# A second gate with its weights in four column groups of TensorE, and expert blocks nested in each other

## The chip, the core and the metric

The kernel runs on one core of one Trainium2 chip. The core has five engines, each with its own queue of instructions: TensorE (PE; PEld is its loading of weights), VectorE (DVE), ScalarE (ACT), GpSimd (POOL) and SyncE (SP, which here issues loads and stores). They wait for each other by semaphores. The metric is the device time of one execution in microseconds, the median of several.

## The reference

Three stages, in f32. First a linear attention over 4 batches, 8 heads, 576 positions and 64 numbers a head. Then a gated layer, and then a mixture of 8 experts, of which each of the 2304 tokens uses one:

```
x = attention(q, k, v)                     # 2304 tokens x 512
x = (sigmoid(x @ w_gate) * (x @ w_val)) @ w_out          # 1536 wide
logits = x @ moe2_w_gate                   # 2304 x 8, the second gate
e = argmax(logits);  g = softmax(logits)[e]
out = g * (relu(x @ w1[e]) @ w2[e])        # 8 experts, 1024 wide
```

An expert takes at most `capacity` tokens, in their order; what comes beyond gets zeros.

## The kernel before

All matmuls that carry much work are made of three in fp32r (a rounded f32): high times high, high times low, low times high (`mm3`, lines 114 to 119). The others (the attention's, the second gate's) are plain f32.

The tokens are worked in six blocks of 384 (`BLK`). In the gated layer TensorE goes through steps; one step multiplies a block by two slices of `w_gate` and `w_val` (tiles `pg` and `pv`), and adds the product of an earlier step with `w_out` (`po`) to the block's row of `acc`. The code's order is the order of each engine's queue (a manual schedule). When a block's rows in `acc` are done, the second gate follows for it:

- `columns` turns a block's three tiles of 128 tokens with TensorE (`pl`), and ScalarE copies them into `w5`, so that the 512 numbers of a token lie along partitions.
- `logits_mm` makes the logits: for each tile of tokens, four matmuls of 128 tokens by 8 experts (`plg`), one for each 128 of the 512 numbers, added up in PSUM. They aren't issued at once: they go into the list `weave`, and each `mm3` takes the first entry of that list when it has issued its own three matmuls. An entry has two of the small matmuls, and three in the last two blocks; the entry behind the last copies the logits to SBUF with VectorE and starts `route`.
- `route` and `route_b` find each token's expert, its place in that expert's list and its gate, and GpSimd scatters these into a table in DRAM.

The sixth block's second gate runs inside the first expert's work, which begins early with the tokens of the first five.

The experts come last, in order of a plan that the kernel computes: those with tokens first. `part` does the work of up to 384 tokens of one expert: gathered rows, turned (`turn`), times `w1` (`ph`), `relu`, times `w2` (`yo`), scaled, and scattered to the output by GpSimd. The loop over the experts after the first is unrolled, each block in a condition:

```
for j in range(1, NE):
    with tc.If(nact > j):
        st, ew = body(j, st, ew)
```

`nact` is the number of experts that have tokens. `body` works the first 256 tokens, in a condition of its own up to 320 more, and brings in the next expert's weights. Each condition is a branch on all five engines. Its false side makes up for what the true side would have done to the semaphores, so that later waits still fit: on GpSimd that is an instruction for the queues of its own DMAs, which shows in the profile as INC_SWDGE_SEM.

Tiles come from pools, which hand out buffers in turn, among them `units`, 13 large ones for weights and rows.

Of the kernel before, what the change touches and what calls it, by code (L numbers as in the profile page):

```python
# [8 lines left out]
F32 = mybir.dt.float32  # L9
F32R = mybir.dt.float32r  # L10
BF16 = mybir.dt.bfloat16
I32 = mybir.dt.int32
AF = mybir.ActivationFunctionType
ALU = mybir.AluOpType
# [4 lines left out]
P = 128  # L19
B, H, S, D = 4, 8, 576, 64  # L20
NT = B * S
DM = H * D
DFF = 1536
NE = 8
FE = 1024
NC = DM // P
NFC = DFF // P
BLK = 384
NBLK = NT // BLK
TPB = BLK // P  # L30
NTILE = NT // P
NUNIT = 13
RA = 256
RB = 320
# [33 lines left out]
go4.0 hl5.1* ac4.2 ac3.2* ac4.0*  # L68
"""
F64_MIN = struct.unpack("<f", struct.pack("<I", 897 << 20))[0]  # L70


def program(tc, ins, outs):
    nc = tc.nc
    ctx = ExitStack()
    with ctx:
# [4 lines left out]
        def unit(shape, dt, name):  # L81
            return units.tile(shape, dt, name=name, tag="unit")

        ident = const.tile([P, P], F32, name="ident", tag="ident")
# [18 lines left out]
        hp = ctx.enter_context(tc.tile_pool(name="hp", bufs=4))  # L103
        stg = ctx.enter_context(tc.tile_pool(name="stg", bufs=2))
        tbp = ctx.enter_context(tc.tile_pool(name="tbp", bufs=2))
        psa = ctx.enter_context(tc.tile_pool(name="psa", bufs=5, space=PSUM))
        pso = ctx.enter_context(tc.tile_pool(name="pso", bufs=3, space=PSUM))

        def ps(name):
            return psa.tile([P, 512], F32, name=name, tag="a")  # L110

        weave = []
# [53 lines left out]
        def gather(st, i, idx, g, n, rows=NT):  # L166
            nc.gpsimd.indirect_dma_start(
                out=g[:n],
                out_offset=None,
                in_=x2d[0:rows],  # L170
                in_offset=bass.IndirectOffsetOnAxis(ap=idx, axis=0),
                bounds_check=rows - 1,
                oob_is_err=False,
            )
            st[i] = g

        def turn(st, i, x, k, n=P):
            g = st.pop(i)
            pt = ps(f"tg{i}").rearrange("p (c t) -> p c t", c=NC)
            for c in range(NC):  # L180
                nc.tensor.transpose(pt[:, c, :n], g[:n, c * P : (c + 1) * P], ident[:n, :n])
            o = k * P
            nc.scalar.copy(x[:, :, 0, o : o + n], pt[:, :, :n])
            nc.vector.tensor_tensor(
                x[:, :, 1, o : o + n], pt[:, :, :n], x[:, :, 0, o : o + n].bitcast(F32), op=ALU.subtract
            )
# [74 lines left out]
        with ExitStack() as s2:  # L261
# [178 lines left out]
            def cb(f, i):  # L440
                tf, mag = ld["c", f, i]
                nc.vector.scalar_tensor_tensor(tf, mag, F64_MIN, tf, op0=ALU.is_ge, op1=ALU.mult)

# [84 lines left out]
            rt = {}  # L528

            def open_routing():  # L530
                s_at.close()
                p = s2.enter_context(tc.tile_pool(name="rt", bufs=1))
                rt["pool"] = p
                rt["wgt"] = wgt = p.tile([P, NC, NE], F32, name="wgt", tag="wgt")
                rt["tokf"] = tokf = p.tile([P, TPB], F32, name="tokf", tag="tokf")
                rt["gidx"] = p.tile([P, 3], I32, name="gidx", tag="gidx")
                rt["rel"] = p.tile([P, TPB], F32, name="rel", tag="rel")
                fill = p.tile([P, NROW // P, 4], I32, name="fill", tag="fill")
                nc.gpsimd.memset(fill, 0)
                nc.gpsimd.iota(fill[:, :, 1], [[1, NROW // P]], base=NT, channel_multiplier=NROW // P)  # L540
                nc.sync.dma_start(tbl.rearrange("(p j) w -> p j w", p=P), fill)
                nc.sync.dma_start(capt, ins["cap"].unsqueeze(0).to_broadcast([P, 2]))
                nc.vector.tensor_copy(capf, capt[:, 0:1])
                nc.sync.dma_start(wgt, ins["wgt"])
                nc.gpsimd.iota(
                    tokf, [[P, TPB]], base=(NBLK - 1) * BLK, channel_multiplier=1, allow_small_or_imprecise_dtypes=True
                )
# [150 lines left out]
            for token in FIRST.split():  # L698
                name = token.rstrip("*")
# [21 lines left out]
            w5 = None  # L721

            def side(b):
                return int(b == 4)
# [8 lines left out]
                    nc.scalar.copy(w5[:, side(b), tt], pt)  # L733

            def logits_mm(b, then):
                rt["lg", b] = rt["pool"].tile([P, TPB, NE], F32, name=f"lg{b}", tag="lg", bufs=2)
                pl = ps(f"plg{b}")

                def one(tt, c):
                    nc.tensor.matmul(  # L740
                        pl[:, tt * NE : (tt + 1) * NE],
                        w5[:, side(b), tt, c * P : (c + 1) * P],
                        rt["wgt"][:, c, :],
                        start=c == 0,
                        stop=c == NC - 1,
                    )

                def end():
                    nc.vector.tensor_copy(rt["lg", b].rearrange("p t e -> p (t e)"), pl[:, : TPB * NE])
                    then()  # L750

                n = 3 if b > 3 else 2
                pairs = [(tt, c) for tt in range(TPB) for c in range(NC)]
                for i in range(0, len(pairs), n):
                    weave.append(lambda i=i: [one(*x) for x in pairs[i : i + n]])
                weave.append(end)

            def first_rows():
# [23 lines left out]
            for b in range(5):  # L782
                k = (4, 5, 7, 9, 11)[b]
# [12 lines left out]
            for i, (b, fs, mode) in enumerate(steps):  # L796
# [7 lines left out]
                k = i % NBLK  # L804
# [18 lines left out]
                if i == n4 + 1:  # L823
                    whole_w(11)
                    w5 = unit([P, 2, TPB, DM], F32, "w5")
# [7 lines left out]
            xb = unit([P, NC, 2, 3 * P], F32R, "xb0")  # L833
# [60 lines left out]
        xgp = s3.enter_context(tc.tile_pool(name="xgp", bufs=2, reuse_waits="tile"))  # L894
        grp = s3.enter_context(tc.tile_pool(name="grp", bufs=7, reuse_waits="tile"))

        def g_tile(i):
            return grp.tile([P, DM], F32, name=f"gr{i}", tag="gr")

        def next_tables(e):  # L900
            st = {}
            fetch(st, "ta", e, 0, 2)
            fetch(st, "tb", e, RA, 2, rest=True)
            for i in range(2):
                gather(st, i, st["ta"][:, i, 0:1], g_tile(i), P)
            return st

        def turn_a(st):
            st["xa"] = xgp.tile([P, NC, 2, RA], F32R, name="xa", tag="xa")
            for i in range(2):  # L910
                turn(st, i, st["xa"], i)
# [4 lines left out]
        def work(ew, e, fs, lag):  # L916
            at = {}
            for i, f in enumerate(fs):
                at.setdefault(0 if i < 2 else lag[i - 2], []).append(lambda f=f: ew_dma(ew, e, f))
                at.setdefault(lag[i], []).insert(0, lambda f=f: ew_split(ew, f, both))  # L920
            return at
# [16 lines left out]
        ew, st = {}, {}  # L938
# [19 lines left out]

        nact = st.pop("nact")

        def body(j, st, ew):
            more = j + 1 < NE
            cj = nc.values_load(plan[0:1, NE + j : NE + j + 1], min_val=0, max_val=NT)
            xb = unit([P, NC, 2, RB], F32R, "xb")
            nst, new = {}, {}

            def extra(f):
                if f == 0:
                    for i in range(3):
                        n = P if i < 2 else HALF  # L970
                        gather(st, 2 + i, st["tb"][:n, i, 0:1], g_tile(2 + i), n)
                if f == 1 and more:
                    nst.update(next_tables(nexp[j]))
                if 4 <= f <= 6:
                    turn(st, f - 2, xb, f - 4, P if f < 6 else HALF)
                if f == 7 and more:
                    turn_a(nst)

            half = work(new, nexp[j], range(4), (2, 4, 5, 6)) if more else {}
            part(st["xa"], RA, (P, P), ew, st["ta"], grp, "gr", *hooks(half, extra))  # L980
            if more:
                for k in (3, 4, 5):
                    new["u", k] = unit([P, 3, 2, 512], F32R, f"eu{k}")
            with tc.If(cj > RA) as big:
                half = work(new, nexp[j], range(4, 8), (1, 3, 5, 6)) if more else {}
                part(xb, RB, (P, P, HALF), ew, st["tb"], grp, "gr", *hooks(half))
            if more:
                with big.Else():
                    half = work(new, nexp[j], range(4, 8), (1, 2, 3, 4))
                    for f in range(5):  # L990
                        for w in half.get(f, ()):
                            w()
            return nst, new

        for j in range(1, NE):
            with tc.If(nact > j):
                st, ew = body(j, st, ew)


def layout(inputs):  # L1000
# [37 lines left out]
```

## Time and profile before

| | |
|---|---|
| three runs | 800.02, 800.99 and 801.18 us, median 800.99 |
| the profiled execution | 800.0 us, its span from first to last instruction 798.2 us |
| TensorE busy | 759.5 us, 95% of the span, 4400 matmul passes |
| VectorE, ScalarE, GpSimd busy | 402.2, 278.8 and 273.2 us |
| TensorE's granted clock | 0.987 of full speed |

The profile lists instructions by line and tile (names without buffer numbers). An f32 matmul shows as two passes. A matmul's recorded length is longer than its share of the time, since several are under way at once: the distance from one start to the next tells what it takes. Branches, semaphore work and drains aren't counted as busy; they have rows of their own under their line, with a q behind the engine (PEldq, POOLq).

### The profile page before, as it was taken

The page shows a single profiled execution, that of the slowest core. Times are in us where ns is not written, and L with a number is a line of the kernel's source. Part 1 is how long each engine was busy: PE and PEld are TensorE (multiplying, and loading weights), DVE is VectorE, ACT ScalarE, POOL GpSimd, SP SyncE. Part 2 cuts the span into 40 slices and gives each one's busy share as a digit, 9 for nine tenths or more (in the row PEclk, how much of TensorE's full clock was granted, in tenths as well). Part 3 has the DMA queues.
Part 4 walks back from the last instruction along what each step waited for, and adds up shares of the span by engine and source line. Part 5 has one row for each costly group of instructions (what it writes and reads, how often), then busy time and mean ns, then how long its engine had stood idle before and what let it go on. Part 6 is the DMA issues. An engine that isn't in the chain of part 4 may idle for free. (4 is left out here: it accounts for less than half of the span.)

```text
span 798.2 us, 11945 instructions
## 1 busy us (share of the span) xinstructions
PE 759.5 (95%) x4400; PEld 698.0 (87%) x4400; DVE 402.2 (50%) x826; ACT 278.8 (35%) x537; POOL 273.2 (34%) x276
## 2 busy tenths in 40 slices
PE   6989999999999999999999999999999999999980
PEld 5988998999999999999989999999888888888870
DVE  7999966345454454544863323347724422433330
ACT  6756833322222222222332112223325533524430
POOL 5473713123232232322331313222535524425220
PEclk9999999999999999999999999999999999999995
DMA  9952020111010110101211011143255524515311
GB/s 305 364 172 83 28 79 28 31 53 53 27 54 27 53 50 31 53 28 53 80 67 40 2 41 41 53 134 117 62 150 176 191 80 127 159 53 182 129 41 37
DMA packets 34798, 70.53 MB, mean 88 GB/s; under 512 B 6528, under 2 KB 8704, under 8 KB 34720
## 3 DMA queue, kind: packets, MB, share of 16 engines
q1 hardware_dynamic: 31008, 59.40, 22.7%
q0 software_dynamic: 3712, 10.13, 4.0%
q8 instruction: 43, 0.70, 0.4%
q14 instruction: 35, 0.29, 0.1%
HBM read 59.45 MB, written 9.55 MB: 86 GB/s over the span
## 5 line engine op out<-in xcount | busy, mean ns | idle before, releaser
L491 POOL TENSOR_TENSOR h<-sg,h 128x384 fp32r<-128x384 f32 x70 | 77.6, 1110 | 242.5 <-ACT h L487 236.3
L483 DVE TENSOR_TENSOR sg<-sg,pv 128x384 f32<-128x384 f32 x72 | 39.7, 553 | 125.3 <-PE pv L117 100.6
L115 PE MATMUL pg<-xT,w 128*128 128x384 f32 x288 | 99.0, 344 | 0.0
L115 PE MATMUL pv<-xT,w 128*128 128x384 f32 x288 | 98.1, 341 | 0.1
L117 PE MATMUL pv<-xT,w 128*128 128x384 f32 x288 | 96.6, 336 | 1.5 <-POOL w L451 1.5
L116 PE MATMUL pg<-xT,w 128*128 128x384 f32 x288 | 96.7, 336 | 0.0
L117 PE MATMUL pg<-xT,w 128*128 128x384 f32 x288 | 96.5, 335 | 0.0
L116 PE MATMUL pv<-xT,w 128*128 128x384 f32 x288 | 96.4, 335 | 0.0
L117 PE MATMUL po<-w,h 128*128 128x512 f32 x216 | 86.0, 398 | 0.0
L115 PE MATMUL po<-w,h 128*128 128x512 f32 x216 | 85.2, 394 | 0.0
L116 PE MATMUL po<-w,h 128*128 128x512 f32 x216 | 85.1, 394 | 0.0
L479 ACT ACTIVATE sg<-pg 128x384 f32<-128x384 f32 x72 | 35.3, 490 | 129.4 <-PE pg L117 129.3
L451 POOL TENSOR_TENSOR w<-cv,w 128x512 fp32r<-128x512 f32 x34 | 45.1, 1325 | 98.7 <-ACT w L447 97.6
L487 ACT CAST h<-sg 128x384 fp32r<-128x384 f32 x68 | 34.9, 514 | 111.5 <-DVE sg L483 107.5
L238 DVE SCALAR_TENSOR_TENSOR h<-ph,h 128x64 fp32r<-128x64 f32 (+2 forms) x96 | 31.1, 354 | 84.0 <-ACT h L235 83.6
L135 POOL TENSOR_TENSOR eu<-es,eu 128x512 fp32r<-128x512 f32 x34 | 44.0, 1302 | 85.8 <-ACT eu L134 77.6
L521 DVE TENSOR_TENSOR acc<-acc,po 128x512 f32<-128x512 f32 x78 | 53.1, 687 | 36.5 <-PE po L117 35.3
L235 ACT ACTIVATE h<-ph 128x256 fp32r<-128x256 f32 (+3 forms) x64 | 26.3, 411 | 98.9 <-PE ph L117 61.0
L135 DVE TENSOR_TENSOR eu<-es,eu 128x512 fp32r<-128x512 f32 x46 | 43.1, 948 | 32.7 <-ACT eu L134 32.3
L117 PEld LDWEIGHTS pv<-xT,w 128*128 128x128 f32 x288 | 54.1, 188 | 2.2 <-POOL w L451 2.2
L116 PEld LDWEIGHTS pg<-xT,w 128*128 128x128 f32 x288 | 54.2, 188 | 1.3
L115 PEld LDWEIGHTS pg<-xT,w 128*128 128x128 f32 x288 | 54.1, 188 | 1.4
(201 smaller groups left out, 1667.9 us busy)
## 6 DMA issues: line engine op xcount, KB each, us to landing
es<-in_w SPq DMA_DIRECT2D x80, 256.0 KB, 3.4
s<-in_w SPq DMA_DIRECT2D x30, 512.0 KB, 3.4
q<-in_q SPq DMA_DIRECT2D x18, 256.0 KB, 7.0
x2d<-acc SPq DMA_DIRECT2D x6, 768.0 KB, 3.6
kt<-in_kT SPq DMA_DIRECT2D x3, 1152.0 KB, 8.1
vt<-in_v SPq DMA_DIRECT2D x3, 1024.0 KB, 15.0
raw<-in_w SPq DMA_DIRECT2D x6, 512.0 KB, 11.3
kt<-in_kT SPq DMA_DIRECT2D x4, 288.0 KB, 4.9
```

Of the source, the lines that this page charges most:

```text
L115: nc.tensor.matmul(out, l_hi, r_hi, start=start, stop=False)
L116: nc.tensor.matmul(out, l_hi, r_lo, start=False, stop=False)
L117: nc.tensor.matmul(out, l_lo, r_hi, start=False, stop=stop)
L135: engines[(i + f) % 2].tensor_tensor(u[:, 1], s[:, i], u[:, 0].bitcast(F32), op=ALU.subtract)
L235: nc.scalar.activation(h[:, 0, :used], ph[:, :used], AF.Relu)
L238: nc.vector.scalar_tensor_tensor(dst, ph[:, cols], 0.0, h[:, 0, cols].bitcast(F32), op0=ALU.max, op1=ALU.subtract)
L451: two[eng].tensor_tensor(w[:, i, 1, :], ld.pop(("c", f, i))[0], w[:, i, 0, :].bitcast(F32), op=ALU.subtract)
L479: nc.scalar.activation(pr, gt.pop(("g", b, f)), AF.Sigmoid)
L483: nc.vector.tensor_tensor(pr, pr, gt.pop(("v", b, f)), op=ALU.mult)
L487: alt[eng](h[:, 0], gt["r", b, f])
L491: two[eng].tensor_tensor(h[:, 1], gt.pop(("r", b, f)), h[:, 0].bitcast(F32), op=ALU.subtract)
L521: nc.vector.tensor_tensor(row(b, tt), row(b, tt), otile[b, tt], op=ALU.add)
```

## The change

In the second gate, weights and rows change places. The eight columns of each quarter of the weights are padded with zeros to 32 and stand in one of four groups of 32 columns of the array; all 384 turned tokens of the block move past them. Four matmuls give four partial sums on 4 x 32 partitions. ScalarE copies them to SBUF, and three matmuls, one for each 128 tokens, with a matrix `pick` of zeros and ones add the four and turn the result back to tokens by experts. In `weave` that is an entry with all four, two empty ones, three with one matmul each, and the last one as before.

The expert blocks are nested: block j + 1 stands inside the condition of block j. For that the pools are replaced, ahead of the blocks, by rings of tiles that are allotted once and handed out in turn (`Ring`), and the weights by two fixed sets of six tiles that alternate; the numbers of buffers stay.

```diff
+class Ring:
+    def __init__(self, tiles):
+        self.tiles, self.n = list(tiles), 0
+
+    def tile(self, shape, dt, name, tag):
+        self.n += 1
+        return self.tiles[(self.n - 1) % len(self.tiles)]
...
-                rt["wgt"] = wgt = p.tile([P, NC, NE], F32, name="wgt", tag="wgt")
+                rt["wgt"] = wgt = p.tile([P, NC, P // NC], F32, name="wgt", tag="wgt")
+                nc.gpsimd.memset(wgt, 0.0)
+                rt["pick"] = pick = p.tile([P, NE], F32, name="pick", tag="pick")
+                nc.vector.tensor_tensor(pick, ident[:, 0:NE], ident[:, 32 : 32 + NE], op=ALU.add)
+                for c in range(2, NC):
+                    nc.vector.tensor_tensor(pick, pick, ident[:, 32 * c : 32 * c + NE], op=ALU.add)
...
-                nc.sync.dma_start(wgt, ins["wgt"])
+                nc.sync.dma_start(wgt[:, :, :NE], ins["wgt"])
...
             def logits_mm(b, then):
                 rt["lg", b] = rt["pool"].tile([P, TPB, NE], F32, name=f"lg{b}", tag="lg", bufs=2)
                 pl = ps(f"plg{b}")
-
-                def one(tt, c):
+                sums = rt["pool"].tile([P, BLK], F32, name=f"lsum{b}", tag="lsum")
+                w = P // NC
+
+                def four():
+                    for c in range(NC):
+                        nc.tensor.matmul(
+                            pl[c * w : (c + 1) * w, :BLK],
+                            rt["wgt"][:, c, :],
+                            w5[:, side(b), :, c * P : (c + 1) * P],
+                            start=True,
+                            stop=True,
+                            tile_position=(0, c * w),
+                        )
+                    nc.scalar.copy(sums, pl[:, :BLK])
+
+                def one(tt):
                     nc.tensor.matmul(
-                        pl[:, tt * NE : (tt + 1) * NE],
-                        w5[:, side(b), tt, c * P : (c + 1) * P],
-                        rt["wgt"][:, c, :],
-                        start=c == 0,
-                        stop=c == NC - 1,
+                        pl[:, BLK + tt * NE : BLK + (tt + 1) * NE],
+                        sums[:, tt * P : (tt + 1) * P],
+                        rt["pick"],
+                        start=True,
+                        stop=True,
                     )
...
-                n = 3 if b > 3 else 2
-                pairs = [(tt, c) for tt in range(TPB) for c in range(NC)]
-                for i in range(0, len(pairs), n):
-                    weave.append(lambda i=i: [one(*x) for x in pairs[i : i + n]])
+                weave.extend([four, lambda: None, lambda: None])
+                weave.extend(lambda tt=tt: one(tt) for tt in range(TPB))
                 weave.append(end)
...
+        sets = [
+            {k: u for k, u in ew.items() if k[0] == "u"},
+            {("u", k): unit([P, 3, 2, 512], F32R, f"ev{k}") for k in range(6)},
+        ]
+        xb1 = unit([P, NC, 2, RB], F32R, "xb1")
+        hp = ring(hp, 4, [P, 2, BLK], F32R, "h")
+        stg = ring(stg, 2, [P, 2, 512], F32, "stg")
+        psa = ring(psa, 5, [P, 512], F32, "a")
+        pso = ring(pso, 3, [P, 512], F32, "o")
+        grp = ring(grp, 7, [P, DM], F32, "gr")
+        xgp = ring(xgp, 1, [P, NC, 2, RA], F32R, "xa", st["xa"])
...
-        for j in range(1, NE):
+        def chain(j, st, ew):
             with tc.If(nact > j):
-                st, ew = body(j, st, ew)
+                nst, new = body(j, st, ew)
+                if j + 1 < NE:
+                    chain(j + 1, nst, new)
+
+        chain(1, st, ew)
```

How TensorE's queue stands at the first block's second gate, before: `pg` and `pv` are the gated layer's matmuls (three rows are one `mm3`), `plg` the logits, each row x2 being one entry of `weave`.

```order
L115 MATMUL pg_8_3724<-xT_770,w_2796 128x384
L116 MATMUL pg_8_3724<-xT_770,w_2796 128x384
L117 MATMUL pg_8_3724<-xT_770,w_2796 128x384
L740 MATMUL plg_3723<-wgt,w_3526 128x8 x2
L115 MATMUL pg_8_3724<-xT_770,w_2796 128x384
L116 MATMUL pg_8_3724<-xT_770,w_2796 128x384
L117 MATMUL pg_8_3724<-xT_770,w_2796 128x384
L740 MATMUL plg_3723<-wgt,w_3526 128x8 x2
```

The same place of TensorE's queue after (the lines are those of the changed kernel; `w` is the tile `w5`, `lsum` the copied partial sums):

```order
L134 MATMUL pg_8_3730<-xT_770,w_2801 128x384
L135 MATMUL pg_8_3730<-xT_770,w_2801 128x384
L136 MATMUL pg_8_3730<-xT_770,w_2801 128x384
L769 MATMUL plg_3728<-w_3531,wgt 32x384 x4
L134 MATMUL pg_8_3730<-xT_770,w_2801 128x384
L135 MATMUL pg_8_3730<-xT_770,w_2801 128x384
L136 MATMUL pg_8_3730<-xT_770,w_2801 128x384
```

All four matmuls stand where the first two stood; two more `mm3` without an insert follow, then one matmul with `pick` behind each of the next three.

The second place is GpSimd's queue at the end of the last but one expert block, before: L984 is the inner condition, L996 the condition on `nact`, and ISA is the instruction for the DMA queues on a false side.

```order
L984 ISA
L984 UNCONDITIONAL_BRANCH
L996 ISA
L996 UNCONDITIONAL_BRANCH
L996 COMPARE_AND_BRANCH
L963 TENSOR_LOAD plan
```

The end of GpSimd's queue after, from the last block's inner condition on (L1039 is the inner condition now, L1051 that on `nact`, L1093 the end):

```order
L1039 ISA
L1039 UNCONDITIONAL_BRANCH
L1051 ISA
L1051 UNCONDITIONAL_BRANCH
L1051 ISA
L1051 UNCONDITIONAL_BRANCH
L1051 ISA
L1051 UNCONDITIONAL_BRANCH
L1051 ISA
L1051 UNCONDITIONAL_BRANCH
```

Before, a false side led to the next block's condition; now the false sides stand together behind the last block, and each ends in a branch to the program's end, so that one of them runs at most.

## Rows read from the trace of the kernel before

**Rows 1.** The page: the span, then each engine's busy us, share and instructions.
```profile
span 798.2 us, 11945 instructions
PE 759.5 (95%) x4400; PEld 698.0 (87%) x4400; DVE 402.2 (50%) x826; ACT 278.8 (35%) x537; POOL 273.2 (34%) x276
```

**Rows 2.** Stretches: from:to, length, busy us of PE, PEld, DVE, ACT, POOL, clock, DMA.
```profile
100.00:200.00 100.00, 99.97 (x541) 92.57 (x540) 53.06 (x86) 30.27 (x57) 26.16 (x25) 1.00 0.15 49
...
650.00:700.00 50.00, 49.75 (x302) 44.04 (x301) 18.59 (x35) 19.80 (x41) 20.26 (x18) 1.00 0.40 125
...
784.50:798.20 13.70, 0.00 (x0) 0.00 (x0) 0.00 (x0) 0.00 (x0) 0.00 (x0) 0.50 0.03 7
```

**Rows 3.** Timeline of the end: start us, length, engine, line, operation.
```profile
775.72 0.39 PE L117 MATMUL yo<-eu,h 128*128 128x512 f32 x1
...
779.48 0.92 POOL L144 DMA_INDIRECT out<-y,tb  x1 [0.30 <-issue]
```

**Rows 4.** Sequencer instructions of L996: count, ns min/median/max, first and last start.
```profile
L996 PEldq COMPARE_BRANCH x7: 70/3825/5667, 610.2 to 788.8; - x7
...
L996 POOLq INC_SWDGE_SEM x4: 1353/1353/1371, 784.4 to 791.0; - x4
```

**Rows 5.** The same view of L1034, the barrier at the program's end.
```profile
L1034 POOLq DRAIN x3: 46/107/4960, 792.4 to 797.9; - x3
...
L1034 PEldq DRAIN x2: 8/8/8, 793.6 to 797.7; - x2
```

**Rows 6.** DMA queues from 784.3 to 798.3: packets, MB, share.
```profile
q8 instruction: 5, 0.08, 3.3%
```

**Rows 7.** The tile plg: its matmul passes, and what they waited for (us, times).
```profile
L740 PE MATMUL plg<-wgt,w x144: 170/256/277, 421.2 to 553.3; 128*128 128x8 f32 x144
...
  ACT w L733: 1.1, 5
```

**Rows 8.** Timeline of TensorE around the first block's gate matmuls.
```profile
420.53 0.42 PE L115 MATMUL pg<-xT,w 128*128 128x384 f32 x1
...
421.21 0.61 PE L740 MATMUL plg<-wgt,w 128*128 128x8 f32 x4
421.68 0.42 PE L115 MATMUL pg<-xT,w 128*128 128x384 f32 x1
...
426.51 0.42 PE L115 MATMUL pv<-xT,w 128*128 128x384 f32 x1
...
427.12 0.33 PE L115 MATMUL pv<-xT,w 128*128 128x384 f32 x1
...
427.64 0.40 PE L115 MATMUL po<-w,h 128*128 128x512 f32 x1
```

**Rows 9.** Timelines of TensorE, ScalarE and VectorE around the last block's.
```profile
549.26 0.36 PE L115 MATMUL ph<-xa,eu 128*128 128x256 f32 x1
...
553.36 0.48 PE L115 MATMUL yo<-eu,h 128*128 128x512 f32 x1
...
554.63 0.28 PE L115 MATMUL ph<-xa,eu 128*128 128x256 f32 x1
...
554.98 0.28 PE L115 MATMUL ph<-xa,eu 128*128 128x256 f32 x1
...
557.22 0.19 PE L590 MATMUL pc<-oh,tri 128*128 128x24 bf16 x1
...
549.55 0.58 ACT L733 COPY w<-pl 128x512 f32<-128x512 f32 x1 [0.29 <-PE pl L729]
...
554.96 0.55 DVE L578 TENSOR_TENSOR run<-run,oh 128x8 bf16<-128x8 bf16 x3
```

**Rows 10.** Timeline of ScalarE around the first block's gate matmuls.
```profile
420.58 1.55 ACT L733 COPY w<-pl 128x512 f32<-128x512 f32 x3
```

**Rows 11.** Timeline of TensorE: plain f32 matmuls with 128 moving columns.
```profile
55.05 2.40 PE L353 MATMUL pkv<-vt,ek 128*128 128x128 f32 x20
57.28 0.60 PE L399 MATMUL pq<-ident,q 128*128 128x128 f32 x4
```

More of the change, by code (lines that the diff above doesn't have):

```diff
@@ L70, with __init__, tile @@
 F64_MIN = struct.unpack("<f", struct.pack("<I", 897 << 20))[0]
+class Ring:
[4 more added lines that the diff above has]
+        return self.tiles[(self.n - 1) % len(self.tiles)]
+class Tables:
+    def __init__(self, ta, tb):
+        self.of = {"ta": ta, "tb": tb}
+    def tile(self, shape, dt, name, tag):
+        return self.of[tag].tile(shape, dt, name, tag)
 def program(tc, ins, outs):
@@ L737, in logits_mm @@
                 pl = ps(f"plg{b}")
-                def one(tt, c):
-                    nc.tensor.matmul(
-                        pl[:, tt * NE : (tt + 1) * NE],
-                        w5[:, side(b), tt, c * P : (c + 1) * P],
-                        rt["wgt"][:, c, :],
-                        start=c == 0,
-                        stop=c == NC - 1,
+                sums = rt["pool"].tile([P, BLK], F32, name=f"lsum{b}", tag="lsum")
[12 more added lines that the diff above has]
+                def one(tt):
+                    nc.tensor.matmul(
+                        pl[:, BLK + tt * NE : BLK + (tt + 1) * NE],
[3 more added lines that the diff above has]
+                        stop=True,
                     )
                 def end():
-                    nc.vector.tensor_copy(rt["lg", b].rearrange("p t e -> p (t e)"), pl[:, : TPB * NE])
+                    nc.vector.tensor_copy(
+                        rt["lg", b].rearrange("p t e -> p (t e)"), pl[:, BLK : BLK + TPB * NE]
+                    )
                     then()
-                n = 3 if b > 3 else 2
-                pairs = [(tt, c) for tt in range(TPB) for c in range(NC)]
-                for i in range(0, len(pairs), n):
-                    weave.append(lambda i=i: [one(*x) for x in pairs[i : i + n]])
+                weave.extend([four, lambda: None, lambda: None])
+                weave.extend(lambda tt=tt: one(tt) for tt in range(TPB))
                 weave.append(end)
@@ L959, in program, with ring @@
         nact = st.pop("nact")
+        def ring(pool, n, shape, dt, tag, *first):
+            more = [pool.tile(shape, dt, name=f"{tag}r{i}", tag=tag) for i in range(n)]
+            return Ring([*more, *first])
+        sets = [
[9 more added lines that the diff above has]
+        xgp = ring(xgp, 1, [P, NC, 2, RA], F32R, "xa", st["xa"])
+        tbp = Tables(ring(tbp, 1, [P, 2, 4], I32, "ta", st["ta"]), ring(tbp, 1, [P, 3, 4], I32, "tb", st["tb"]))
         def body(j, st, ew):
@@ L963, in body @@
             cj = nc.values_load(plan[0:1, NE + j : NE + j + 1], min_val=0, max_val=NT)
-            xb = unit([P, NC, 2, RB], F32R, "xb")
-            nst, new = {}, {}
+            xb = xb1
+            nst, new = {}, dict(sets[j % 2])
             def extra(f):
@@ L980, in body @@
             part(st["xa"], RA, (P, P), ew, st["ta"], grp, "gr", *hooks(half, extra))
-            if more:
-                for k in (3, 4, 5):
-                    new["u", k] = unit([P, 3, 2, 512], F32R, f"eu{k}")
             with tc.If(cj > RA) as big:
```

## The prediction

> **What bounds the kernel now.** I read the page first, then the stretches, the instructions of the engines' sequencers by line, the timeline around the first block of gate matmuls, and the tile of the logits. The page gives TensorE 95% of the span [rows 1]. By stretches, it has no free time in the middle (99.97 of 100 us) nor in the expert stage (49.75 of 50), while no engine at all is busy from 784.5 to 798.2 [rows 2]. So a microsecond counts in two places only: what TensorE itself executes or waits for, and the dead end behind the last scatter. All else (VectorE is at 53 of 100 us, GpSimd at 26) has cover [rows 2].
>
> The end explains itself by line. TensorE's last matmul starts at 775.72 and GpSimd's last scatter at 779.48, over at 780.4 [rows 3]. Of the seven conditions at L996 the last four are false, one after the other (one INC_SWDGE_SEM each). GpSimd pays for each an INC_SWDGE_SEM of 1.35 us, the first at 784.4, the fourth at 791.0: (791.0 − 784.4) / 3 = 2.2 us from one to the next [rows 4]. TensorE jumps over a body each time too, with branches of 3.8 us (median) to 5.7, the last at 788.8 [rows 4], so that it gets to its final drain at 793.6 [rows 5]; 16 KB instruction packets still arrive in that time [rows 6]. GpSimd gets to its own drain at 792.4, and that one takes 4.96 us [rows 5]: 797.4, and 0.8 us later the span ends. GpSimd is the later of the two.
>
> **The change, part by part.** *Nested blocks.* After the change the first false condition jumps to the end of the program. The order shows the four INC_SWDGE_SEM that run now become one, since each false side has its own, which ends in a branch to the end. The first cannot come earlier than today, because the order has it waiting for the scatters' queues, as now. Then the drain follows at 784.4 + 1.35 = 785.75 instead of 792.4: −6.6 us. TensorE's one jump instead of four starts where today's first does, about its last matmul, and should be over by 782 at the 5.7 us of the longest, and still before GpSimd if it took 10: today's four together end at 793.6. The drain itself is the unknown: it could shrink with the number of INC_SWDGE_SEM before it (4.96 / 4 = 1.24 us each, so 3.7 less), to almost nothing (46 ns is GpSimd's shortest [rows 5]), or stay. I take it as it is, since its long form stands once in the trace and nothing there ties it to the count.
>
> *Rings and fixed weight tiles.* They hand out the same number of buffers in the same turn, and the expert stage's matmuls stay the same ones. I cost them at nothing; what hides them is that TensorE is full there (49.75 of 50), and the bound is the 0.25 us per 50 us that it idles, about 1 us in the whole stage either way.
>
> *Zeroed weights, 0/1 matrix.* One GpSimd fill and three small VectorE additions at about 144 us, under a TensorE with 99.97 of 100 us [rows 2]: nothing. SyncE's load of the weights now waits for that fill, but the queue's DMA ahead of it waits for a fill of GpSimd already. Without cover it would be a microsecond once.
>
> *The gate matmuls before.* 72 matmuls with 8 moving columns are 144 passes, since an f32 matmul is two passes [rows 7]: 24 in each of six blocks. In the first block six groups of four passes lie between groups of three pg/pv matmuls. A group of three alone takes 427.64 − 427.12 = 0.52 us; from 420.53 to 426.51 there are six groups and six inserts, 5.98 us [rows 8]. So the block costs 5.98 − 6 × 0.52 = 2.85 us. From 421.68 to 426.51 it is 4.83 − 5 × 0.52 = 2.23 us for 20 passes: 0.11 a pass. In the last block (groups of 0.35 us with 256 columns, four inserts) it is 553.36 − 549.26 − 4 × 0.35 = 2.70 us [rows 9].
>
> *The gate matmuls after.* Four terms.
>
> First a new wait. The old first insert needs one copied tile of turned rows; the new four matmuls read all three. TensorE reaches that place at about 421.1, but ScalarE's three copies are done at 420.58 + 1.55 = 422.13 [rows 8, 10]. Five blocks find even the first copy barely done (1.1 us of waits in five cases [rows 7]), so all five wait some 1.05 us; in the last block the third copy ends at 550.13, and TensorE is there at 549.61: 0.55 us [rows 9]. Everything of TensorE is queued behind, and as it is the bound, all that comes later is late by as much.
>
> Second, the four matmuls: eight passes of 384 moving columns in f32. Such a pass isn't in the trace. The nearest is pkv, 128 columns: (57.28 − 55.05) / 20 = 0.1115 us [rows 11], three times that for 384 is 0.334 us. Below, a 384-column pass in fp32r is 0.52 / 3 = 0.174 [rows 8]. How far the four column groups overlap no row shows either. One after the other: 8 × 0.334 = 2.67 us. Wholly side by side: 2 × 0.334 = 0.67. In between: passes start in order, and the second pass of a matmul must wait for the first of its own column group, but may run beside the first pass of the next group; that makes five slots, 1.67 us. I take this one: two passes in a row on one group is what the f32 matmuls look like now.
>
> Third, going back from 32-column groups to the whole array: I allow one emptying of the array, the recorded length of a 384-column matmul less its pace, 0.33 − 0.17 = 0.16 us [rows 8]; going in is free, as the array is empty after the wait. Below it is nothing.
>
> Fourth, three additions by the 0/1 matrix, two passes each of 8 columns at 0.11: 0.67 us. They stand three groups (1.56 us) behind the four; ScalarE's copy of the sums needs about 0.7 of that, and ScalarE has nothing else queued ahead of it, so no wait.
>
> Together: 1.05 + 1.67 + 0.16 + 0.67 = 3.55 us against 2.85, +0.70 in five blocks; 0.55 + 1.67 + 0.16 + 0.67 = 3.05 against 2.70, +0.35 in the sixth. The new gate costs 5 × 0.70 + 0.35 = **+3.9 us**. In the sixth block the logits come two groups later, 0.7 us at 0.35 a group; the routing behind them ends at 555.51 now and TensorE asks for it at 557.22 [rows 9], so 1.7 us hide that. With the cover gone it would cost up to 0.7 us once.
>
> *Sum.* +3.9 − 6.6 = −2.7 us on the span, 798.2 to 795.5. The profiled execution took 800.0 us, the median of the runs 800.99; I put the difference on the median: **798.3 us**.
>
> On the overlap the Trainium skill (TensorE: Matmul & The Clock Gate, "Measured speedup vs the span model") states a rule: matmuls in different column groups take the time of one plus about 4 ns each, 2.38 times faster for three. No run here shows it. By it the four would take two passes' time, which is the third rival below. Its page TensorEngine Tiling (Array Packing), "Key Properties", says that a change of tiling mode drains the engine; by that the third term stands, and the sum would not differ.
>
> **The rivals.** (A) The forecast: five slots, the drain as it is. 798.3 us.
>
> (B) No overlap of column groups in f32: the four take 2.67 us, 1.0 more in each of six blocks, +6.0: the gate +9.9, the total +3.3, **804.3 us**, slower. It decides from 2.12 us per four on, where the gate eats the 6.6 of the end (2.7 / 6 = 0.45 above 1.67). For it: two passes in a row on one group and double reading of f32; against it: nothing in the trace.
>
> (C) Full overlap: 0.67 us, the gate −2.1, the total −8.7, **792.3 us**. Against it: the two passes of one matmul stand one behind the other in the instruction order.
>
> (D) GpSimd's drain shrinks with the INC_SWDGE_SEM: 3.7 less, the total −6.4, **794.6 us**. For it: the drain is long only where these precede it; against it: each of them has signalled before the next starts (2.2 us apart, 1.35 long).
>
> (E) The nested skip saves nothing, because the single INC_SWDGE_SEM, which stands for four experts, takes four times as long, or TensorE's jump over four bodies does: +3.9, **804.9 us**. Against it: an instruction adds to counters, whatever the amount.
>
> **How the numbers follow.** Chances: A 0.38, B 0.24, C 0.14, D 0.15, E 0.05, something else 0.04. The range goes from D to B, 794.3 to 804.6, which leaves out C and E, about 0.2; that of A alone is 797 to 800. A measurement of this kernel tells 0.2%, 1.6 us. A lies 2.7 below, so about seven in ten of it count as faster; C and D wholly. Faster: 0.27 + 0.14 + 0.15 + 0.01 = 0.57; B mostly and E count as slower: 0.20 + 0.05 = 0.25; the rest, 0.18, within.
>
> **What would show it.** In the profile after: one INC_SWDGE_SEM at the line of the nested condition, and GpSimd's drain starting some 5.4 us after the last scatter's end (780.4 to 785.75) instead of 12, 5 us long (right) or short (D). In the gate: TensorE idle some 1 us ahead of the four, for ScalarE's copies; from the first of the four to the next pg matmul 1.7 to 1.9 us (A), 2.7 (B) or 0.7 to 0.9 (C). I would be wrong in the reasons if TensorE had no wait for the third copy, if the expert stage had new waits from the rings, or if TensorE's jump and not GpSimd ended last.

## The result, and the profile after

The changed kernel took 788.37 us (median of four runs, 787.09 to 789.89) beside 801.09 us for the kernel before: a ratio of 0.984, 95% interval [0.981, 0.987]. Faster was right; 798.3 us and the range 794.3 to 804.6 were not. The profiled execution took 788.12 us, so the comparison by traces is 798.2 to 786.3 us of span. Medians below are of all executions of a kernel; the ratios leave out two slow ones, of 2667 us (`nest_only`) and 940 us (`late_four`).

The page after:

```profile
span 786.3 us, 11792 instructions
...
PE 752.0 (96%) x4340; PEld 686.1 (87%) x4340; DVE 402.7 (51%) x829; ACT 281.6 (36%) x543; POOL 274.6 (35%) x277
```

Against [rows 1] TensorE runs 60 passes (and 60 weight loads) fewer. Next, the timeline of TensorE, first and last block, in the columns of [rows 8, 9]:

```profile
421.32 0.42 PE L134 MATMUL pg<-xT,w 128*128 128x384 f32 x1
...
421.75 0.34 PE L136 MATMUL pg<-xT,w 128*128 128x384 f32 x1
422.97 0.85 PE L769 MATMUL plg<-w,wgt 128*32 128x384 f32 x8 [0.88 <-ACT w L757]
423.76 0.44 PE L134 MATMUL pg<-xT,w 128*128 128x384 f32 x1
...
425.44 0.28 PE L780 MATMUL plg<-pick,lsum 128*128 128x8 f32 x2
425.58 0.42 PE L134 MATMUL pv<-xT,w 128*128 128x384 f32 x1
...
428.21 0.40 PE L134 MATMUL po<-w,h 128*128 128x512 f32 x1
...
549.13 0.28 PE L136 MATMUL ph<-xa,eu 128*128 128x256 f32 x1
549.73 0.85 PE L769 MATMUL plg<-w,wgt 128*32 128x384 f32 x8 [0.32 <-ACT w L757]
550.51 0.39 PE L134 MATMUL ph<-xa,eu 128*128 128x256 f32 x1
```

The wait for ScalarE's third copy is there: from the last pg matmul to the four, 1.22 us instead of a matmul's pace of 0.17 (from one start to the next), so 1.05 us. The four matmuls, eight passes, take 0.79 us in all until the next pg matmul starts. All told, from the first pg to the first po it is 6.89 us, against 7.11 [rows 8].

The end, as in [rows 3 to 5]: the timeline, then the sequencers' instructions of the nested condition (L1051) and of the program's end (L1093):

```profile
772.19 0.39 PE L136 MATMUL or<-eu,hr 128*128 128x512 f32 x1
...
775.68 0.92 POOL L163 DMA_INDIRECT out<-grr,tb  x1 [0.30 <-issue]
```

```profile
L1051 POOLq INC_SWDGE_SEM  x1: 1370/1370/1370, 778.9 to 778.9; - x1
...
L1093 POOLq DRAIN  x3: 46/107/4962, 780.5 to 786.0; - x3
...
L1093 PEldq DRAIN  x2: 8/8/8, 774.4 to 785.8; - x2
```

One INC_SWDGE_SEM instead of four; GpSimd's drain of 4.96 us as before; TensorE is at its own drain at 774.4, long before GpSimd.

By stages (from the first transposes of a block, `pl`, and the last matmul in the two timelines):

| stage | before | after | difference |
|---|---|---|---|
| start to the first `pl` | 419.30 | 420.09 | +0.79 |
| first to sixth `pl` (five gates) | 128.73 | 127.49 | −1.24 |
| sixth `pl` to the last matmul (a gate, the expert stage) | 227.69 | 224.61 | −3.08 |
| last matmul to the end | 22.50 | 14.09 | −8.41 |

### The profile page after: what moved, and what is told of

It is laid out like the page before. It is cut to its first block, busy times and chain, and to the rows that moved or that the text cites. A ratio compares the mean times of both kernels' runs of the same rounds, so it can differ in the third digit from the quotient of the medians.

```text
span 786.3 us, 11792 instructions
## 1 busy us (share of the span) xinstructions
PE 752.0 (96%) x4340; PEld 686.1 (87%) x4340; DVE 402.7 (51%) x829; ACT 281.6 (36%) x543; POOL 274.6 (35%) x277
## 4 chain that ended last, share of the span: by engine, by line
PE 76%; DVE 8%; issue 6%; ACT 4%; DMA 2%; POOL 2%; SPq 1%; POOLq 0%; ACTq 0%; DVEq 0%
PE po L136 6%; PE po L135 6%; PE po L134 6%; PE pv L134 6%; PE pv L136 6%; PE pv L135 6%; PE pg L134 6%; PE pg L135 5%; PE pg L136 5%; PE ar L134 2%; PE ar L136 2%; PE ar L135 2%; PE or L134 2%; PE or L135 2%; PE or L136 2%
## 5 line engine op out<-in xcount | busy, mean ns | idle before, releaser
L257 DVE SCALAR_TENSOR_TENSOR hr<-ar,hr 128x64 fp32r<-128x64 f32 (+1 forms) x72 | 23.5, 354 | 80.3 <-ACT hr L254 80.3
L134 PEld LDWEIGHTS pg<-xT,w 128*128 128x128 f32 x288 | 54.1, 188 | 4.5 <-issue 3.1
L136 PEld LDWEIGHTS pv<-xT,w 128*128 128x128 f32 x288 | 54.1, 188 | 2.3 <-POOL w L470 2.3
L135 PEld LDWEIGHTS pg<-xT,w 128*128 128x128 f32 x288 | 54.1, 188 | 1.3
L134 PEld LDWEIGHTS pv<-xT,w 128*128 128x128 f32 x288 | 54.2, 188 | 0.6 <-issue 0.4
L135 PEld LDWEIGHTS pv<-xT,w 128*128 128x128 f32 x288 | 54.2, 188 | 0.0
L136 PEld LDWEIGHTS pg<-xT,w 128*128 128x128 f32 x288 | 54.1, 188 | 0.0
## 6 DMA issues: line engine op xcount, KB each, us to landing
raw<-in_w SPq DMA_DIRECT2D x6, 512.0 KB, 11.6
```

The source lines that it names most:

```text
L134: nc.tensor.matmul(out, l_hi, r_hi, start=start, stop=False)
L135: nc.tensor.matmul(out, l_hi, r_lo, start=False, stop=False)
L136: nc.tensor.matmul(out, l_lo, r_hi, start=False, stop=stop)
L257: nc.vector.scalar_tensor_tensor(dst, ph[:, cols], 0.0, h[:, 0, cols].bitcast(F32), op0=ALU.max, op1=ALU.subtract)
```

## The experiments

Unless it is said otherwise, the ratio is to the kernel before in the same series, with its 95% interval. In the first series of four the kernel before itself ranged from 799.0 to 807.6 us, so the times there say little; three of its kernels were run again in a later one.

### The two halves alone

The gate alone (the new `logits_mm`, zeroed weights and `pick`, and the old loop, pools and conditions), and the nested blocks, rings and weight tiles alone with the old gate:

```diff
 gate_only, gate_only_2: before.py with
+    weave.extend([four, lambda: None, lambda: None])
+    weave.extend(lambda tt=tt: one(tt) for tt in range(TPB))
 nest_only, nest_only_2: before.py with
+    hp = ring(hp, 4, [P, 2, BLK], F32R, "h")
...
+    chain(1, st, ew)
```

> Only the new gate; expert blocks, pools and conditions as before. If the four matmuls of the four column groups overlap (0.79 us for all, as the trace after has it): each of five blocks 0.2 to 0.3 us shorter, the gate -1.4 us, 799.5 us, with the end as before (22 us from the last matmul to the end). If the gate costs what was predicted (3.55 us a block): 805. If the 3 us that the expert stage lost after the change came from the gate: 796.5 and no stall of TensorE at about 580 us.

> Only the nested blocks, rings and fixed weight tiles; the gate as before. By the prediction -6.6 us, 794.4. If the 8.4 us of the end and the 3 us of the expert stage both come from here: 789.7, with 14 us from the last matmul to the end and no 2 us gap of TensorE at about 580. If the expert stage gained by chance of where instruction packets fall: between the two, with other gaps than either trace shows.

Measured: 805.17 us (1.004 [1.001, 1.007]) and 800.29 us (0.997 [0.994, 1.000]). In both traces the gate and the end are as in the traces of before and after (five gates 127.5 us with the new gate, 128.7 with the old; the end 21.6 us with four conditions, 15.0 nested), and the expert stage is 6 to 7 us longer, with waits of TensorE of up to 4 us at the borders of expert blocks and stretches at half the clock. These times can't be read as the price of an edit, so both went again:

> Only the new gate, once more (the first time the kernel before itself was up to 7 us longer in some runs of its series than in others). If the gate gives 1.3 us and the 2 us gap at about 580 goes with it: 797, last matmul some 3 us earlier than before, the end as before. If the expert stage's waits of the first time (9 us) belong to this kernel: 805 again.

> Only the nested blocks and rings, once more. If the end is all that they change: 8 us less than before, 792 to 793, the last matmul where it was. If the waits of 4 to 7 us at the borders of expert blocks belong to this kernel: 800 again.

Measured: gate alone 797.39 us (0.996 [0.995, 0.998]), nested alone 793.50 us (0.992 [0.990, 0.993]). GpSimd's instructions at the old conditions in the first, at the nested one in the second:

```profile
L1017 POOLq INC_SWDGE_SEM  x4: 1353/1353/1371, 779.9 to 786.6; - x4
```

```profile
L1030 POOLq INC_SWDGE_SEM  x1: 1374/1374/1374, 786.2 to 786.2; - x1
```

Gate alone: five gates 127.49 us again, and no gap at 580. Nested alone: last matmul 778.78, end 793.6, so 14.8 us; its stage after the sixth `pl` is 2.8 us longer than before, and two stretches at half the clock account for 3.4 and up to 1.7 us of lost work, the second 3.4 us long, at 566.9. The first (columns of [rows 2]):

```profile
553.30:560.10 6.80, 6.80 (x26) 5.81 (x26) 3.63 (x15) 1.63 (x4) 0.00 (x0) 0.50 0.64 193
```

The granted clock is 0.50, the level of 1.2 GHz, with TensorE busy before and in it. The parts give −2.8 and −6.7 us, the whole −11.6 (`after_again` below): within the intervals they add up. The gate gains, against the forecast: 1.24 of its 2.8 us in the five gates, the rest behind them, where the gap at 580 is part of it (below).

### The four matmuls in one column group

```diff
 one_group: after.py with
-    pl[c * w : (c + 1) * w, :BLK],
+    pl[:w, :BLK],
...
-    start=True,
-    stop=True,
-    tile_position=(0, c * w),
+    start=c == 0,
+    stop=c == NC - 1,
+    tile_position=(0, 0),
...
-    nc.scalar.copy(sums, pl[:, :BLK])
+    nc.scalar.copy(sums[:w], pl[:w, :BLK])
...
-    sums[:, tt * P : (tt + 1) * P],
-    rt["pick"],
+    sums[:w, tt * P : (tt + 1) * P],
+    ident[:w, :NE],
```

> The changed kernel, but the four matmuls all go to the first group of 32 columns and add up there; the three behind use 32 rows of an identity. Same number of instructions and columns. If column groups run side by side in f32: the four take eight passes one behind the other, 8 x 0.17 to 0.33 us = 1.4 to 2.7 us instead of 0.79, six times: 3.5 to 11 us slower than the changed kernel, 792 to 799. If they don't overlap and a pass is simply short (0.1 us): the same as the changed kernel, 788.4.

Measured: 820.16 us (1.020 [1.017, 1.024]). TensorE in the first block:

```profile
422.69 2.77 PE L769 MATMUL plg<-w,wgt 128*32 128x384 f32 x8 [0.88 <-ACT w L757]
425.39 0.45 PE L134 MATMUL pg<-xT,w 128*128 128x384 f32 x1
...
426.89 0.34 PE L136 MATMUL pg<-xT,w 128*128 128x384 f32 x1
427.16 0.38 PE L780 MATMUL plg<-ident,lsum 32*128 32x8 f32 x2
427.47 0.44 PE L134 MATMUL pv<-xT,w 128*128 128x384 f32 x1
```

425.39 − 422.69 = 2.70 us for the same eight passes, 0.34 a pass, against 0.79 in four groups: the overlap is shown. The matrix of 32 rows costs more too: 0.27 us from the matmul ahead to it and 0.31 from it to the next, 0.17 and 0.14 with `pick`'s 128 rows.

The time itself is 21 us above the 799 that was expected at most. The five gates take 141.28 us instead of 127.49, so 2.76 us a block: 1.91 for the four, and about 0.8 for the three additions, which the expectation did not count. Six blocks make some 16.5 of the 31 to 32 us over the changed kernel. The other half is not in the gate: the trace has it in the expert stage, with waits of TensorE of 2.96 and 3.98 us and 13.7 us at half the clock, as in the other kernels of this series.

The Trainium skill (TensorE: Matmul & The Clock Gate, "Measured speedup vs the span model") has matmuls in different column groups take the time of one plus about 4 ns each. The trace agrees to about 0.1 us: two passes of 0.34 us are 0.67, against 0.79 until the next matmul of the whole array starts.

### The four matmuls later

```diff
 late_four, late_four_2: after.py with
+    weave.extend([lambda: None] * (2 if b < NBLK - 1 else 1))
     weave.extend([four, lambda: None, lambda: None])
```

> The changed kernel with the four matmuls two entries later in the order (one in the last block), 1.05 us of other matmuls more between ScalarE's copies and them. If the wait for the third copy is a real cost: it goes in five blocks, -1.05 us each and -0.35 in the sixth, 782.8 us. If something else is late next (the sums' copy, the routing): the wait shows up at another line and the time stays at 788.

Measured: 795.38 us (0.991 [0.988, 0.994]), not 782.8, with the five gates at 122.8 us instead of 127.5. What was won by the sixth block went in the expert stage, in stretches such as these (TensorE idle, then at half the clock):

```profile
671.90:674.20 2.30, 0.00 (x0) 0.00 (x0) 0.00 (x0) 0.00 (x0) 1.01 (x1) 0.99 0.50 138
674.20:681.00 6.80, 6.16 (x23) 5.48 (x24) 2.23 (x4) 2.28 (x5) 1.28 (x1) 0.50 0.37 111
```

> The changed kernel with the four matmuls two entries later, once more. The first trace had the wait gone and five blocks 4.7 us shorter in all, then 12 us lost at the borders of expert blocks. If those waits are not this kernel's: 783 to 784. If they are: 795 again.

Measured: 785.38 us (0.981 [0.979, 0.983]), the fastest here. It is clearly ahead of the kernel before; the changed kernel's medians are 3 and 4 us above it, but in other series and with intervals that overlap or touch its own, and in the first series this kernel took 795.38. TensorE in its first block, and a stretch of its expert stage:

```profile
421.79 0.34 PE L136 MATMUL pg<-xT,w 128*128 128x384 f32 x1
422.06 0.85 PE L769 MATMUL plg<-w,wgt 128*32 128x384 f32 x8
422.84 0.45 PE L134 MATMUL pg<-xT,w 128*128 128x384 f32 x1
```

```profile
557.50:560.90 3.40, 3.40 (x13) 2.69 (x14) 2.53 (x10) 0.00 (x0) 1.87 (x3) 0.50 0.02 5
```

No wait is left at the four (0.27 us from the matmul ahead, 0.10 over the pace); five gates take 122.82 us, 4.67 less than in the changed kernel. By the ratios of these two series some 3.4 us of that stay (0.981 against 0.986 for the changed kernel, below, of 800 us). The trace shows where the rest can go: 3.4 us at half the clock cost 1.7 (13 passes, where the next 3.0 us at full clock hold 22), and there is a later wait of 1.6 us for VectorE.

### Both kernels once more

> The changed kernel once more, unaltered, beside the kernel before in the same series. If the expert stage's 3 us were gained by the change: from the last block of turned rows to the last matmul 224 to 225 us again, and 788. If that stage varies by itself from run to run (waits of TensorE of 1 to 4 us at the borders of expert blocks, as the two parts made alone showed): 228 us or more, and some 792 to 796.

> The kernel before once more, unaltered. If its one 2 us gap of TensorE at about 580 us belongs to its code: it stands again at the same place. If it came from one late packet: it is gone or elsewhere, and the expert stage is longer or shorter by as much. The end (last matmul to the end of the span) 22 us either way.

Measured: 789.44 us (0.986 [0.983, 0.988]) and 800.01 us (0.999 [0.998, 1.000]). The stage after the sixth `pl` is 225.50 us in the one (224.61 in the first trace) and 227.88 in the other (227.69), and the trace of before has its gap again, from 580.23 to 582.12. So the gap belongs to the program and is no accident of one execution.

### Rings without nesting, and no false conditions

```diff
 rings_before: nest_only.py with
-    chain(1, st, ew)
+    for j in range(1, NE):
+        with tc.If(nact > j):
+            st, ew = body(j, st, ew)
 three: before.py with
-    for j in range(1, NE):
+    for j in range(1, 4):
```

> Rings and fixed weight tiles, but the conditions one after the other as before, and the gate as before. If rings cost and bring nothing: as the kernel before, 801, with four INC_SWDGE_SEM of GpSimd at the end and 22 us there. If the expert stage's 3 us or the shorter end come from the rings: 2 to 3 us less.

> The kernel before with the loop over experts cut to the three that are active here: the conditions that come out false and their blocks are left out of the program (right for these inputs only). If the end is the price of the false conditions: no INC_SWDGE_SEM at that line behind the last scatter, GpSimd's drain right after the scatters have landed, about 13 us from the last matmul to the end, 792. If the drain shrinks when nothing of the kind stands before it: 8 to 9 us, 787.

Measured: rings 800.45 us (0.999 [0.998, 1.000]), so in sum they bring and cost nothing, with 21.5 us at the end; in their trace the gap at 580 is gone, and 3.4 us at half the clock (566 to 569) take about as much. Without false conditions 789.07 us (0.985 [0.983, 0.987]), and 10.1 us at the end (last matmul 778.22, span 788.4), between the two that were expected, 13 and 8 to 9; its last matmul is 2.5 us later than before, with the gap at 580 and 3.4 us at half the clock. The last scatter and the program's end in that kernel:

```profile
781.62 0.92 POOL L144 DMA_INDIRECT out<-y,tb  x1 [0.30 <-issue]
```

```profile
L1034 POOLq DRAIN  x3: 46/113/6564, 780.9 to 788.1; - x3
```

With no INC_SWDGE_SEM in the way the drain starts at 780.9, while the last scatters are still under way, and is over at 787.5, which is 4.97 us after the last scatter's end: the drain's price is the same as elsewhere, only that nothing stands between. In the changed kernel (14.1 us) it starts only behind the one INC_SWDGE_SEM, which waits for the landing: in all six traces with such an instruction where the profile has the last scatter's landing, the first one starts 0.29 us after it. So the false conditions cost 12 us of end, of which nesting takes 8 away, and the last of them still costs 4.

### The same work, its instructions further along

The changed kernel has 120 instructions of TensorE fewer ahead of the expert stage. The Trainium skill (Runtime: NRT & Kernel Launch, "Instruction fetch mechanics") says that instructions come in blocks of 16 KiB, 256 instructions, by the sequencer's own DMA queue, at a cost that is mostly hidden. By it 136 more shift the borders as 120 fewer do.

```diff
 shift: before.py with, ahead of all other matmuls
+    shift = ps("shift")
+    for i in range(68):
+        nc.tensor.matmul(shift[:32, :8], tri[:, :32], tri[:, :8], start=True, stop=True)
```

> The kernel before with 68 tiny matmuls (136 instructions of TensorE with their weight loads) put ahead of its first, in TensorE's idle first 8 us: the same work, its instruction stream 136 instructions further along. If the gap at about 580 us comes from a 16 KB instruction packet that TensorE's place in the stream fetches just as the table's scatter lands (573 to 578): the packet falls elsewhere, the table's load comes 2.1 us after the third scatter instead of 4.7, the 2 us gap goes, 799. If the gap belongs to the work itself: it stays, 801.

Measured: 799.06 us (0.9986 [0.9971, 1.0001]), as expected, though this interval alone settles nothing, since it holds 1 as well. The traces tell the two apart. Before, the DMA queues from 573 to 578.5, then the timelines of SyncE, VectorE and TensorE:

```profile
q8 instruction: 1, 0.02, 2.1%
...
tbl<-ent,si POOLq DMA_INDIRECT x1, 4.7
```

```profile
577.92 0.33 SPq L160 DMA_DIRECT2D tb<-tbl  x1
...
581.00 0.68 DVE L219 TENSOR_TENSOR y<-y,z 64x512 f32<-64x512 f32 x1 [4.65 <-DMA z<-y]
...
580.11 0.40 PE L116 MATMUL yo<-eu,h 128*128 128x512 f32 x1
582.21 0.50 PE L117 MATMUL yo<-eu,h 128*128 128x512 f32 x1 [1.70 <-DVE h L238]
```

The same in `shift`:

```profile
tbl<-ent,si POOLq DMA_INDIRECT x1, 2.1
```

```profile
575.15 0.33 SPq L163 DMA_DIRECT2D tb<-tbl  x1
...
578.36 0.68 DVE L222 TENSOR_TENSOR y<-y,z 64x512 f32<-64x512 f32 x1 [2.13 <-DMA z<-y]
```

The chain is: a 16 KB instruction packet on queue q8 runs while the table's last scatter lands, which then takes 4.7 us instead of 2.1; SyncE's load of the table waits for it, the load of `z` stands behind that, VectorE's addition waits for `z`, the split of `h` stands behind the addition, and TensorE waits for `h`. With the stream shifted no q8 packet falls into these 5.5 us (the packet of 574.87 is now at 565.38, the next at 585.16), and the 2 us gap is gone. The second trace of before has the packet and a landing after 4.43 us; the kernel without false conditions has both too (4.42 us) and the gap at 582; in the five other traces where this landing is on record no packet runs beside the scatter for more than its last 0.1 us, and it takes 2.1 us. After the sixth `pl` `shift` takes 225.93 us, 1.76 less than before with the same work, though the next wait, for ScalarE's `h` at 597 to 600, is 1.50 us in it against 0.48 and 1.19 in the two traces of before. The changed kernel's stage, less its gate's 0.65, is 1.5 and 2.4 us shorter in its two traces, with no packet on the scatter and no gap at 580 in either: the same effect. Of the page's "mostly hidden" in the Trainium skill this case shows another side: TensorE's supply didn't stop, but the scatter beside the packet was late.

## Why the prediction was wrong

**Nested blocks: the step held, its size was too small.** One INC_SWDGE_SEM is left, the drain is unchanged at 4.96 us, and from the first INC_SWDGE_SEM to the drain it is 1.57 us instead of 8.05: −6.5 against −6.6. Rival D, the drain that shrinks, falls: 4.96 with one as with four. Rival E falls too: the one that stands for four experts takes 1.37 us, and TensorE is at its drain at 774.4. What was missed: from the last scatter's end to the first INC_SWDGE_SEM it was 3.97 us before (780.40 to 784.4) and is 2.3 now (776.60 to 778.9). "The first cannot come earlier than today" was wrong by 1.7 us: it does wait for the scatters, but the last of them lands earlier. That the instruction packets of TensorE's jumps hold up the landing, as a packet does at 573, fits all traces, but no run moved these packets alone. The queues from the last matmul on, before:

```profile
q8 instruction: 2, 0.03, 3.3%
...
out<-y,tb POOLq DMA_INDIRECT x3, 4.6
```

and after:

```profile
q8 instruction: 1, 0.02, 1.3%
...
out<-grr,tb POOLq DMA_INDIRECT x3, 4.3
```

(the times are medians of those scatters whose landing is on record). For the last scatter alone, from its issue to its landing (or, where that is not on record, to 0.29 us before the first INC_SWDGE_SEM), it is 2.6 us without false conditions, where no packet comes; 2.9 to 3.6 us in the seven traces of nested kernels, with one packet between the last matmul and the landing; and 3.9 to 4.6 us in the six with four false conditions in a row, with two.

**The gate's first term held**: 1.05 us of wait in five blocks (1.22 less the pace of 0.17), 0.48 in the sixth against 0.55. `late_four` took it away by moving the four, and the five gates became 4.67 us shorter.

**The second term is the step that failed.** The "five slots, 1.67 us", with the third term's 0.16 (1.83), measured 0.79, of which some 0.1 (an estimate: 0.79 less two passes) is the way back to the whole array. The pass was sized rightly (0.34 us, shown in one column group); the premise "the second pass of a matmul must wait for the first of its own column group" may hold, but "two passes in a row on one group is what the f32 matmuls look like now" was a reading of matmuls that fill the whole array, and said nothing of groups. Full overlap, as in rival C (chance 0.14), is what happens. This is 1.04 us in each of six blocks, 6.2 in all.

**The fourth term held**: in the first block the three additions cost 0.69 us against 0.67 (four groups from 424.92 to 427.69 take 2.77, less 4 × 0.52). So a block costs 1.05 + 0.79 + 0.69 and some 0.1 of slower pace behind the four, 2.63 instead of 2.85; the sixth 0.48 + 0.78 + 0.69 + 0.1 = 2.05 instead of 2.70; the gate gives 1.24 + 0.65 = 1.9 us. Rival C had 2.1. So the forecast's direction, faster, came right through the end alone: the gate had the wrong sign.

**Rings and fixed weight tiles, costed "at nothing", held; "the expert stage's matmuls stay the same ones" did not suffice.** Same work, but TensorE's instructions stand elsewhere in their stream, and one 16 KB packet no longer falls on the table's scatter: 1.5 to 2.4 us, above the bound of 1 us given for the stage. The prediction bounded the stage by TensorE's idle time and left out that a DMA can be late because of the instructions' own packets.

The sum: predicted span 795.5; less 5.8 for the gate, 1.8 for the end, 2.4 for the expert stage, plus 0.8 for a later start, is 786.3, the span measured.

Open: why in the first series TensorE waited 3 to 4 us at borders of expert blocks in four kernels (five such waits, each with the granted clock at 0.50 for 3.4 or 6.8 us from about its end on), and why the granted clock fell to 0.50 for 3.4 to 6.8 us between 553 and 570 in some traces (nested alone, rings alone, no false conditions, the four later) and in none of before, after, gate alone and `shift`. In the second trace of nested alone TensorE was wholly busy ahead of it (8.30 of 8.30 us from 545).

## What to carry to other kernels

Where f32 matmuls are split over column groups as here, cost them as one group's time, and spend the thought on what feeds them: a wait for the last of several copies cost more than the matmuls, and two empty places in the order removed it. Here a run of false conditions at the program's end was paid one by one by GpSimd, which runs an INC_SWDGE_SEM for each; nested, the first false one leaves. And when a stall sits behind a small DMA that is late in one kernel and not in its variant, look at what else the queues carried in those microseconds before blaming the edit: instructions travel there too. Finally, one series can mislead: three kernels here were 6.8 to 10 us slower in one series than in another, so look at a trace's waits and clock before reading a time as the price of an edit.

## What the hardware showed that was not expected

- Eight f32 passes of 384 columns: 2.70 us in one column group, 0.79 in four.
- A 16 KB instruction packet beside a scatter: 4.7 and 4.4 us to landing instead of 2.1, in both traces of the same program at the same place, and 4.4 in the kernel without false conditions.
- GpSimd's drain ran while scatters were landing where no INC_SWDGE_SEM stood ahead of it: 6.56 us, of which 4.97 after the last scatter's end, over 9.3 us after the last matmul. Behind one or four of them it took 4.96 us from there and was over 13.2 and 21.7 us after it.
- With 136 more instructions of TensorE, in its idle time at the program's start, its last matmul came 1.9 us earlier (traces of `shift` and before).
- The first INC_SWDGE_SEM starts 0.29 us after the last scatter's landing, in six traces of six.
